# Weights of the first mixture rounded on GpSimd instead of ScalarE, with half of their low parts, a unit's third division, and later writes of constant rows

## The chip, the cores and the metric

The kernel runs on one core of one Trainium2 chip. The metric is the device time of one execution in microseconds. A core has five engines with queues of their own, each worked off in order: TensorE (PE in the rows; PEld is its weight load), VectorE (DVE), ScalarE (ACT), GpSimd (POOL) and SyncE (SP), which issues nearly all DMAs here.

## The reference

Attention with a causal mask and a bias from running sums, 4 batches of 8 heads, 576 tokens, head size 64; then two feed-forward layers ("mixtures") on 2304 tokens, 512 to 2048 to 512. Shortened:

```python
def _attn_ref(q, k, v, s) -> np.ndarray:
    B, H, S, D = q.shape
    scale = 1.0 / np.sqrt(D)
    scores = scale * np.matmul(q, k.transpose(0, 1, 3, 2))
    causal = np.triu(np.ones((S, S), dtype=bool), k=1)
    s_pos = np.maximum(s, 0.0)
    cum = np.cumsum(s_pos, axis=-1)
    bias = -(cum[:, :, :, None] - cum[:, :, None, :])
    scores = np.where(causal, -1000000000.0, scores + np.minimum(bias, 0.0))
    scores = scores - np.max(scores, axis=-1, keepdims=True)
    attn = np.exp(scores)
    attn = attn / (np.sum(attn, axis=-1, keepdims=True) + 1e-09)
    return np.matmul(attn, v).astype(np.float32)
...
    x = np.ascontiguousarray(attn_out.transpose(0, 2, 1, 3)).reshape(B * S, H * D)
    h = x @ w_in                                    # first mixture
    x = (h * (1.0 / (1.0 + np.exp(-1.702 * h)))) @ w_out
    h = x @ w_in2                                   # second mixture
    r = np.maximum(h, 0.0)
    return (s2 * (r * r) + b2) @ w_out2
```

The weights `w_in`, `w_out` and so on arrive as 8-byte numbers.

## The kernel before

**Products in parts.** Each fp32 operand of a product is split in a rounded part and a rest ("low part"), both in a type that the TensorE multiplies in one pass; a product is then three: low by rounded, rounded by low, rounded by rounded. The scores and values of the first eight heads alone are multiplied in plain fp32.

**Weights.** A weight tile is 128 x 512 numbers; there are 16 of `wi` (f = 0 to 15) and 16 of `wo` for each mixture. `fetch_w` brings one as 8-byte words (512 KB) on SyncE's queue; `join_w` makes one 4-byte number of the two words, with one instruction on ScalarE (L139) and two on VectorE (L140 with one input, L141 with two); `split_w` rounds it (L149) and takes the low part (L150). `load_w` is all three, for the first mixture. The first mixture's `wi` is loaded two tiles after each attention step while the first eight heads run; its `wo` through a pool of three places (tag "pair").

**Units.** A batch's rows are cut at 320: a unit is one batch's first 320 rows (units 0 to 3) or last 256 rows (4 to 7), with 8 heads. Unit 0's heads (n below H = 8) are done first, alone. Then `run` does the mixture of a unit while it mixes in, at fixed places of the TensorE's order, the attention of the next unit: for a head the score products of up to three chunks of rows (`qk`, L277), a step later the transposes of the probabilities (`transposes`, L315), a step later the product with the values (`pv`, L336 or L342).

**A head.** `qk` takes the maxima on VectorE (L283) from PSUM, the exponentials on ScalarE (L289), reciprocals of the sums on VectorE (L293, L294), and then divides the chunks `x`: all but the last on GpSimd, the last on ScalarE. From head 8 on, `prep` splits a head's queries and keys into `hi` and `lo` (L254 to L257: ScalarE, VectorE, and the keys' low part on GpSimd, L257), with one buffer for `lo`, and the values (L262 and L263). The rows beside queries and keys, four for each, carry the running sums and constants. The first head gets them straight from SBUF; the others from a DRAM tile `rows_d`, which `setup` writes: `minus` and `root` hold constants, `high` and `low` the parts of the running sums.

**The mixture of a unit.** `split_x` splits the four tiles of a unit's x (L390, L391). `h_item` sums a tile of h (L404), with three PSUM places, takes tanh (L425, ScalarE), multiplies (L426, VectorE), rounds `g` (L430, ScalarE) and takes its low part (L431, GpSimd). `th` has two places. `y_item` multiplies `wo` and `g` (L444) for f = 0 to 7 and, later, 8 to 15. For unit 0 three h tiles are begun before the last head's `pv`.

**What sets the order.** The TensorE's order is written out (`attention_items` and `run`), and SyncE's in `setup` and the first eight heads. All other queues are ordered by a scheduler when the kernel is built; each engine then keeps that order. SyncE's issues take turns on eight semaphores, so an issue also waits for the one eight before it.

Of the kernel before, what the change touches and what calls it, by code (L numbers as in the profile page):

```python
# [12 lines left out]
AF = mybir.ActivationFunctionType  # L13
ALU = mybir.AluOpType
# [24 lines left out]
def f32(ap):  # L39
    return ap.bitcast(F32)  # L40
# [27 lines left out]
def fused_kernel(ctx: ExitStack, tc: tile.TileContext, qkT, vP, s, w1i, w1o, w2i, w2o, s2, b2, out):  # L68
    nc = tc.nc
    B, H, _, _ = qkT.shape  # L70
# [10 lines left out]
    first, second = [(0, 64), (64, 192), (192, 320)], [(320, 448), (448, 576)]  # L81
# [18 lines left out]
    rows_d = dram.tile([2, BH, 4, S], F32, name="rows_d")  # L100
# [7 lines left out]
    def scaled(engine, out, in_, scale=1.0):  # L108

        if engine is nc.scalar:  # L110
            nc.scalar.activation(out, in_, AF.Copy, scale=scale)
        elif engine is nc.gpsimd:
            nc.gpsimd.tensor_scalar(out=out, in0=in_, scalar1=scale, scalar2=0.0, op0=ALU.mult, op1=ALU.add)  # L113
        else:
            nc.vector.tensor_scalar(out=out, in0=in_, scalar1=scale, scalar2=None, op0=ALU.mult)  # L115

    def fetch_w(stage, src, f):

        pool, stage_tag, bufs = stage
        if src.dtype == F32:  # L120
            single = pool.tile([P, 2 * CM], F32, tag=stage_tag, name="single", bufs=bufs)[:, :CM]
            nc.sync.dma_start(single, src[f])
            return single
        pair = pool.tile([P, 2 * CM], U32, tag=stage_tag, name="pair", bufs=bufs)
        nc.sync.dma_start(pair, src[f].bitcast(U32))
        return pair

    def join_w(came):

        if came.dtype == F32:  # L130
            return came
        else:

            lower, upper = came[:, 0 : 2 * CM : 2], came[:, 1 : 2 * CM : 2]
            nc.scalar.activation(f32(upper), f32(upper), AF.Prelu, scale=2.0**-112, alpha=2.0**32)  # L139
            nc.vector.tensor_scalar(out=lower, in0=lower, scalar1=2.0**-29, scalar2=7.49, op0=ALU.mult, op1=ALU.min)  # L140
            nc.vector.scalar_tensor_tensor(  # L141
                out=lower, in0=upper, scalar=3, in1=lower, op0=ALU.logical_shift_left, op1=ALU.bitwise_or
            )
            return f32(lower)

    def split_w(single, tag, f):

        w = wp.tile([P, 2, CM], F32R, tag=tag, name=f"{tag}{f}")
        nc.scalar.activation(w[:, 0, :], single, AF.Copy)  # L149
        nc.vector.tensor_tensor(w[:, 1, :], single, f32(w[:, 0, :]), ALU.subtract)  # L150
        return w

    def load_w(stage, src, tag, f):
        return split_w(join_w(fetch_w(stage, src, f)), tag, f)


    with ExitStack() as p1:
# [15 lines left out]
        def setup():  # L173
            cum = gp.tile([P, 2 * NMAX], F32, tag="g", name="cum")[:BH, :S]
            nc.sync.dma_start(cum, s)
            root = gp.tile([P, 2 * NMAX], F32, tag="g", name="root")[:BH, :S]
            nc.gpsimd.memset(root, ROOT)
            minus = gp.tile([P, 2 * NMAX], F32, tag="g", name="minus")[:BH, :S]
            nc.gpsimd.memset(minus, -ROOT)
            prep_to(0)  # L180
            u, t = units[0], heads[0]
            raw = t["parts"][0][0]
            nc.sync.dma_start(raw[D + 2 : R, t["kc"]], minus[:2, : u.i1])
            nc.sync.dma_start(raw[D : D + 2, t["qc"]], root[:2, u.i0 : u.i1])
            for k in range(2):
                nc.sync.dma_start(rows_d[0, :, 2 + k, :], minus)
                nc.sync.dma_start(rows_d[1, :, k, :], root)
            zero = gp.tile([P, 2 * NMAX], F32, tag="g", name="zero")[:BH, :S]
            nc.vector.memset(zero, 0.0)
            pos = gp.tile([P, 2 * NMAX], F32, tag="g", name="pos")[:BH, :S]  # L190
            nc.vector.tensor_scalar(out=pos, in0=cum, scalar1=0.0, scalar2=None, op0=ALU.max)
            nc.vector.tensor_tensor_scan(cum, pos, zero, 0.0, ALU.add, ALU.add)
            high = gp.tile([P, 2 * NMAX], F32R, tag="g", name="high")[:BH, :S]
            nc.vector.tensor_copy(high, cum)
            low = gp.tile([P, 2 * NMAX], F32R, tag="g", name="low")[:BH, :S]
            nc.vector.tensor_tensor(low, cum, f32(high), ALU.subtract)

            for queue, k, part in ((nc.sync, 0, high), (nc.scalar, 1, low)):
                queue.dma_start(raw[D + k : D + k + 1, t["kc"]], f32(part)[:1, : u.i1])
                queue.dma_start(raw[D + 2 + k : D + 3 + k, t["qc"]], f32(part)[:1, u.i0 : u.i1])  # L200
            for k, part in enumerate((high, low)):
                nc.sync.dma_start(rows_d[0, :, k, :], f32(part))
                nc.sync.dma_start(rows_d[1, :, 2 + k, :], f32(part))

        ap, limit = None, 0
        size = {}
# [12 lines left out]
        def tile(shape, name, dtype=F32):  # L219
            return ap.tile([P, *shape], dtype, tag=name, name=name, bufs=size["bufs"][name])  # L220
# [45 lines left out]
        def qk(n, c):  # L266
            u, t = units[n // H], heads[n]
            a0, a1 = u.chunks[c]
            w = a1 - a0
            x = t["x"][c] = tile([size["keys"]], "x")  # L270
            pieces = [(0, a1)] if a1 <= 512 else [(0, a1 // 2), (a1 // 2, a1)]
            least = LARGEST
            for j0, j1 in pieces:
                ps = psS.tile([P, 512], F32, tag="s", name="ps")
                q0, k0 = t["qc"].start - u.i0, t["kc"].start
                for i, (part, rows) in enumerate(t["parts"]):
                    nc.tensor.matmul(  # L277
                        ps[:w, : j1 - j0], part[:rows, q0 + a0 : q0 + a1], part[:rows, k0 + j0 : k0 + j1],
                        start=(i == 0), stop=(i == len(t["parts"]) - 1),
                    )  # L280
                m = sp.tile([P, 1], F32, tag="m", name="m")

                nc.vector.tensor_tensor_reduce(  # L283
                    out=x[:w, j0:j1], in0=ps[:w, : j1 - j0], in1=mask[:w, WIDE - a0 + j0 : WIDE - a0 + j1],
                    scale=-1.0 / ROOT, scalar=least, op0=ALU.add, op1=ALU.min, accum_out=m[:w],
                )
                least = m[:w]
            tot = tots[n % len(tots)]
            nc.scalar.activation(x[:w, :a1], x[:w, :a1], AF.Exp, bias=least, scale=-1.0, accum_out=tot[:w, c : c + 1])  # L289
            last = len(u.chunks) - 1  # L290
            if c < last:
                return
            nc.vector.tensor_scalar(out=tot[:, : c + 1], in0=tot[:, : c + 1], scalar1=1e-9, scalar2=None, op0=ALU.add)  # L293
            nc.vector.reciprocal(tot[:, : c + 1], tot[:, : c + 1])  # L294
            for k, (b0, b1) in enumerate(u.chunks):
                engine = nc.scalar if k == last else nc.gpsimd
                scaled(engine, t["x"][k][: b1 - b0, :b1], t["x"][k][: b1 - b0, :b1], tot[: b1 - b0, k : k + 1])

        def transposes(n, g):
# [71 lines left out]
        def prep_to(n):  # L371
            while n_prep[0] <= min(n, limit - 1):
                prep(n_prep[0])
                n_prep[0] += 1

        def attend(item):
            _, kind, n, k = item
            if kind == "qk":
                if k == 0:
                    prep_to(n + 1)  # L380
                qk(n, k)
            elif kind == "t":
                transposes(n, k)
            else:
                pv(n)
# [252 lines left out]
    def split_next():  # L638
        k = n_split[0]
        if k < len(joined) - 1 or k == len(order) - 1:  # L640
            _, tag, f = order[k]
            (wi2 if tag == "wi" else wo2)[f] = split_w(joined[k], tag, f)
            n_split[0] += 1
            fetch_to(k + 1 + FETCHED)
# [68 lines left out]
```

## Time and profile before

| | us |
|---|---|
| median of 3 runs | 1056.9 (1056.1 to 1056.94) |
| span of the profiled execution | 1052.8 |
| TensorE busy in the span | 1015.6 (96%) |
| VectorE, ScalarE, GpSimd busy | 650.6, 535.8, 347.7 |

The profiled execution's own time isn't listed apart from its span; the median lies 4.1 us above the span, for what comes ahead of the first instruction and behind the last. A row of the timeline gives start, length, engine, line, operation, names of output and inputs and, in brackets, how long the engine had been idle and what ended that. Rows of the same kind that follow each other are merged ("x2").

### The profile page before, as it was taken

To read this page: it belongs to the slowest core of one execution; us is meant where nothing else is said; L and a number is where in the kernel's file an instruction comes from. 1 tells how busy PE (TensorE), PEld (TensorE's weight loads), DVE (VectorE), ACT (ScalarE), POOL (GpSimd) and SP (SyncE) were. 2 spreads that over 40 slices of the span, in tenths; PEclk is the share of its full clock that TensorE was granted. 3 is DMA by queue.
4 is the path that set the end of the run, shared out by engine and by line. 5 is a ranking of instruction groups with operands and counts; after the bars stand their busy time and mean duration, and the time that the engine had idled before them with its cause. 6 is when DMAs were issued, how large, how long until landed. Compare 5 with 4: busy or idle time off the path is not lost.

```text
span 1052.8 us, 17330 instructions
## 1 busy us (share of the span) xinstructions
PE 1015.6 (96%) x6216; PEld 909.6 (86%) x6216; DVE 650.6 (62%) x1441; ACT 535.8 (51%) x1252; POOL 347.7 (33%) x382
## 2 busy tenths in 40 slices
PE   5989999999999999999999999999999999999998
PEld 3459989999989999999999999788888888888887
DVE  4689877567467788778877579866422332232343
ACT  4888856646536646656656557544422322222222
POOL 1126535435335436435445235112410301111011
PEclk9998999999999999999999999999999999999999
DMA  5665331221042232222222084531300100100010
GB/s 178 217 236 182 120 97 56 65 81 44 6 129 71 67 105 72 83 92 72 84 74 68 21 300 134 167 101 41 110 1 1 65 1 1 46 1 1 1 40 21
DMA packets 39181, 85.51 MB, mean 81 GB/s; under 512 B 5660, under 2 KB 16536, under 8 KB 39096
## 3 DMA queue, kind: packets, MB, share of 16 engines
q1 hardware_dynamic: 38888, 84.27, 25.1%
q8 instruction: 49, 0.80, 0.3%
q14 instruction: 36, 0.29, 0.1%
q10 hardware_dynamic: 208, 0.13, 0.0%
HBM read 70.29 MB, written 10.03 MB: 76 GB/s over the span
## 4 chain that ended last, share of the span: by engine, by line
PE 78%; DVE 11%; ACT 4%; DMA 3%; issue 2%; SPq 1%; DVEq 0%; ACTq 0%
PE py L604 19%; PE ph L554 18%; PE py L444 14%; PE ph L404 14%; PE ps L277 4%; PE pst L315 4%; PE po L342 3%; DVE hi L115 3%; DMA pair<-w1i 2%; DVE x L283 1%; PE py L580 1%; ACT x L289 1%; DVE pair L141 1%; DVE pair L140 1%; PE po L336 1%
## 5 line engine op out<-in xcount | busy, mean ns | idle before, releaser
L404 PE MATMUL ph<-xT,wi 128*128 128x320 f32 (+1 forms) x1536 | 246.1, 305 | 5.6 <-ACT xT L390 2.5
L404 PEld LDWEIGHTS ph<-xT,wi 128*128 128x128 f32 x1536 | 217.0, 193 | 7.1 <-ACT xT L390 3.0
L444 PE MATMUL py<-g,wo 128*128 128x320 f32 (+1 forms) x1344 | 215.2, 304 | 0.0
L604 PE MATMUL py<-wo,g 128*128 128x512 f32 x864 | 208.1, 390 | 2.4 <-POOL g L563 2.4
L554 PE MATMUL ph<-xT,wi 128*128 128x512 f32 (+1 forms) x960 | 208.4, 368 | 0.0
L554 PEld LDWEIGHTS ph<-xT,wi 128*128 128x128 f32 x960 | 169.0, 188 | 31.0
L604 PEld LDWEIGHTS py<-wo,g 128*128 128x128 f32 x864 | 161.1, 188 | 36.2 <-POOL g L563 3.3
L444 PEld LDWEIGHTS py<-g,wo 128*128 128x128 f32 x1344 | 188.0, 189 | 0.9 <-POOL g L431 0.2
L558 DVE TENSOR_TENSOR r<-r 128x512 f32<-128x512 f32 (+1 forms) x80 | 53.6, 670 | 189.1 <-ACT r L557 188.9
L431 POOL TENSOR_TENSOR g<-th,g 128x320 fp32r<-128x320 f32 (+1 forms) x128 | 116.3, 909 | 128.9 <-ACT g L430 114.2
L563 POOL TENSOR_TENSOR g<-r,g 128x512 fp32r<-128x512 f32 (+1 forms) x40 | 48.6, 1216 | 306.3 <-PE py L604 174.9
L289 ACT ACTIVATE x<-x,m 64x64 f32<-64x64 f32 (+2 forms) x160 | 89.5, 560 | 100.2 <-DVE m L283 98.8
L557 ACT ACTIVATE r<-ph 128x512 f32<-128x512 f32 (+1 forms) x80 | 44.4, 555 | 147.7 <-PE ph L554 146.1
L257 POOL TENSOR_TENSOR lo<-raw,hi 64x576 fp32r<-64x576 f32 (+1 forms) x56 | 68.1, 1217 | 123.0 <-issue 57.2
L283 DVE CUSTOM_DVE_ANT_0 x<-ps,mask 64x64 f32<-64x64 f32 (+2 forms) x160 | 68.1, 426 | 52.2 <-PE ps L277 50.4
L315 PE MATMUL pst<-ident,x 128*128 128x128 f32 (+2 forms) x480 | 85.8, 287 | 9.9 <-DVE ph L324 8.1
L562 ACT ACTIVATE g<-r 128x512 fp32r<-128x512 f32 (+1 forms) x80 | 47.1, 589 | 91.9 <-DVE r L559 91.8
L113 POOL TENSOR_SCALAR x<-x,tot 64x64 f32<-64x64 f32 (+1 forms) x96 | 49.3, 520 | 91.3 <-DVE tot L294 71.4
L321 ACT ACTIVATE ph<-pst 64x256 fp32r<-64x256 f32 (+2 forms) x144 | 67.0, 473 | 20.6 <-PE pst L315 19.2
L315 PEld LDWEIGHTS pst<-ident,x 128*128 128x128 f32 (+2 forms) x480 | 54.8, 136 | 24.7 <-DVE ph L324 13.0
L425 ACT ACTIVATE th<-ph 128x320 f32<-128x320 f32 (+1 forms) x128 | 51.7, 404 | 45.5 <-PE ph L404 42.7
L426 DVE SCALAR_TENSOR_TENSOR th<-th,ph 128x320 f32<-128x320 f32 (+1 forms) x128 | 57.5, 449 | 22.5 <-ACT th L425 21.5
(71 smaller groups left out, 1334.8 us busy)
## 6 DMA issues: line engine op xcount, KB each, us to landing
raw<-qkT SPq DMA_DIRECT2D x32, 416.0 KB
pair<-w1o SPq DMA_DIRECT2D x16, 512.0 KB
pair<-w1i SPq DMA_DIRECT2D x16, 512.0 KB
pair<-w2i SPq DMA_DIRECT2D x16, 512.0 KB
pair<-w2o SPq DMA_DIRECT2D x16, 512.0 KB
raw<-qkT SPq DMA_DIRECT2D x24, 320.0 KB
vraw<-vP SPq DMA_DIRECT2D x16, 320.0 KB
out<-y SPq DMA_DIRECT2D x17, 256.0 KB
```

Source lines behind the costliest of these rows:

```text
L257: nc.gpsimd.tensor_tensor(lo[:D, kc], raw[:D, kc], f32(hi[:D, kc]), ALU.subtract)
L283: nc.vector.tensor_tensor_reduce(out=x[:w, j0:j1], in0=ps[:w, : j1 - j0], in1=mask[:w, WIDE - a0 + j0 : WIDE - a0 + j1], scale=-1.0 / ROOT ...
L289: nc.scalar.activation(x[:w, :a1], x[:w, :a1], AF.Exp, bias=least, scale=-1.0, accum_out=tot[:w, c : c + 1])
L315: nc.tensor.transpose(ps[: j1 - j0, at : at + a1 - a0], t["x"][c][: a1 - a0, j0:j1], ident[: a1 - a0, : a1 - a0])
L321: nc.scalar.activation(t["ph"][:rows, base:end], ps[:rows, :m], AF.Copy)
L404: nc.tensor.matmul(ph[:, :n], wi[f][:, a, cc * P : (cc + 1) * P], x[cc][:, b, :n], start=(k == 0), stop=(k == 3 * NC - 1),)
L426: nc.vector.scalar_tensor_tensor(out=th[:, :n], in0=th[:, :n], scalar=1.0, in1=ph[:, :n], op0=ALU.add, op1=ALU.mult)
L431: nc.gpsimd.tensor_tensor(g[:, 1, :n], th[:, :n], f32(g[:, 0, :n]), ALU.subtract)
L444: nc.tensor.matmul(py[:, :n], wo[f][:, a, wc], g_t[ui, f][:, b, :n], start=(k == 0), stop=(k == 3 * G - 1))
L554: nc.tensor.matmul(ph[:, :n], wi2[f][:, a, wc], x[cc][:, b, :n], start=(k == 0), stop=(k == 3 * NC - 1))
L558: nc.vector.tensor_tensor(r, r, r, ALU.mult)
L604: nc.tensor.matmul(py[t], g2[k][a][:, t * P : (t + 1) * P], wo2[k][:, b, :], start=(k == 0 and i == 0), stop=(k == NF - 1 and i == 2),)
```

## The change

`split_w` takes a pair of engines. For the first mixture `load_w` hands it GpSimd for the rounding of every tile, and for the low part GpSimd where f is odd and VectorE where it is even. The second mixture's calls keep ScalarE and VectorE. For heads below 8 the third division of `qk` goes to GpSimd too. The four writes of constant rows to `rows_d` move behind those of `high` and `low`, two after each.

```diff
--- before.py
+++ after.py
@@ -143,15 +143,16 @@
             )
             return f32(lower)
 
-    def split_w(single, tag, f):
+    def split_w(single, tag, f, engines=(nc.scalar, nc.vector)):
 
         w = wp.tile([P, 2, CM], F32R, tag=tag, name=f"{tag}{f}")
-        nc.scalar.activation(w[:, 0, :], single, AF.Copy)
-        nc.vector.tensor_tensor(w[:, 1, :], single, f32(w[:, 0, :]), ALU.subtract)
+        first, rest = engines
+        scaled(first, w[:, 0, :], single)
+        rest.tensor_tensor(w[:, 1, :], single, f32(w[:, 0, :]), ALU.subtract)
         return w
 
     def load_w(stage, src, tag, f):
-        return split_w(join_w(fetch_w(stage, src, f)), tag, f)
+        return split_w(join_w(fetch_w(stage, src, f)), tag, f, (nc.gpsimd, nc.gpsimd if f % 2 else nc.vector))
 
 
     with ExitStack() as p1:
@@ -182,9 +183,6 @@
             raw = t["parts"][0][0]
             nc.sync.dma_start(raw[D + 2 : R, t["kc"]], minus[:2, : u.i1])
             nc.sync.dma_start(raw[D : D + 2, t["qc"]], root[:2, u.i0 : u.i1])
-            for k in range(2):
-                nc.sync.dma_start(rows_d[0, :, 2 + k, :], minus)
-                nc.sync.dma_start(rows_d[1, :, k, :], root)
             zero = gp.tile([P, 2 * NMAX], F32, tag="g", name="zero")[:BH, :S]
             nc.vector.memset(zero, 0.0)
             pos = gp.tile([P, 2 * NMAX], F32, tag="g", name="pos")[:BH, :S]
@@ -201,6 +199,8 @@
             for k, part in enumerate((high, low)):
                 nc.sync.dma_start(rows_d[0, :, k, :], f32(part))
                 nc.sync.dma_start(rows_d[1, :, 2 + k, :], f32(part))
+                nc.sync.dma_start(rows_d[0, :, 2 + k, :], minus)
+                nc.sync.dma_start(rows_d[1, :, k, :], root)
 
         ap, limit = None, 0
         size = {}
@@ -293,7 +293,7 @@
             nc.vector.tensor_scalar(out=tot[:, : c + 1], in0=tot[:, : c + 1], scalar1=1e-9, scalar2=None, op0=ALU.add)
             nc.vector.reciprocal(tot[:, : c + 1], tot[:, : c + 1])
             for k, (b0, b1) in enumerate(u.chunks):
-                engine = nc.scalar if k == last else nc.gpsimd
+                engine = nc.scalar if k == last and n >= H else nc.gpsimd
                 scaled(engine, t["x"][k][: b1 - b0, :b1], t["x"][k][: b1 - b0, :b1], tot[: b1 - b0, k : k + 1])
 
         def transposes(n, g):
```

In SyncE's row this is what stands between the constants of the first head and the last write to `rows_d`, before:

```order
L183 DMA raw_119<-minus_117 2x320
L184 DMA raw_119<-root_115 2x320
L186 DMA rows_d_81<-minus_117 32x576
L187 DMA rows_d_81<-root_115 32x576
L186 DMA rows_d_81<-minus_117 32x576
L187 DMA rows_d_81<-root_115 32x576
L199 DMA raw_119<-high_134 1x16x20
L200 DMA raw_119<-high_134 1x16x20
L202 DMA rows_d_81<-high_134 32x576
L203 DMA rows_d_81<-high_134 32x576
L202 DMA rows_d_81<-low_136 32x576
L203 DMA rows_d_81<-low_136 32x576
```

and now:

```order
L184 DMA raw_119<-minus_117 2x320
L185 DMA raw_119<-root_115 2x320
L197 DMA raw_119<-high_130 1x16x20
L198 DMA raw_119<-high_130 1x16x20
L200 DMA rows_d_81<-high_130 32x576
L201 DMA rows_d_81<-high_130 32x576
L202 DMA rows_d_81<-minus_117 32x576
L203 DMA rows_d_81<-root_115 32x576
L200 DMA rows_d_81<-low_132 32x576
L201 DMA rows_d_81<-low_132 32x576
L202 DMA rows_d_81<-minus_117 32x576
L203 DMA rows_d_81<-root_115 32x576
```

The sends of `high` to the first head have moved ahead of all writes to `rows_d`; two of the four constant writes are now the last.

VectorE, from the first of the last four `wi` tiles that come (wi12 to wi15, `pair_587`, `595`, `620`, `628`) to the last x tile of unit 0 (`xT_681`), before, the last 12 rows of 18:

```order
L140 TENSOR_SCALAR pair_620<-pair_620 128x512
L141 SCALAR_TENSOR_TENSOR pair_595<-pair_595 128x512
L140 TENSOR_SCALAR pair_628<-pair_628 128x512
L141 SCALAR_TENSOR_TENSOR pair_620<-pair_620 128x512
L150 TENSOR_TENSOR wi12_592<-pair_587,wi12_592 128x512
L141 SCALAR_TENSOR_TENSOR pair_628<-pair_628 128x512
L150 TENSOR_TENSOR wi13_600<-pair_595,wi13_600 128x512
L150 TENSOR_TENSOR wi14_625<-pair_620,wi14_625 128x512
L140 TENSOR_SCALAR pair_759<-pair_759 128x512
L150 TENSOR_TENSOR wi15_633<-pair_628,wi15_633 128x512
L141 SCALAR_TENSOR_TENSOR pair_759<-pair_759 128x512
L391 TENSOR_TENSOR xT_681<-xraw_607,xT_681 128x320
```

and now, all of it:

```order
L140 TENSOR_SCALAR pair_587<-pair_587 128x512
L151 TENSOR_TENSOR wo0_689<-pair_684,wo0_689 128x512
L141 SCALAR_TENSOR_TENSOR pair_587<-pair_587 128x512
L140 TENSOR_SCALAR pair_595<-pair_595 128x512
L151 TENSOR_TENSOR wo2_740<-pair_735,wo2_740 128x512
L141 SCALAR_TENSOR_TENSOR pair_595<-pair_595 128x512
L140 TENSOR_SCALAR pair_620<-pair_620 128x512
L151 TENSOR_TENSOR wi12_592<-pair_587,wi12_592 128x512
L141 SCALAR_TENSOR_TENSOR pair_620<-pair_620 128x512
L140 TENSOR_SCALAR pair_628<-pair_628 128x512
L141 SCALAR_TENSOR_TENSOR pair_628<-pair_628 128x512
L391 TENSOR_TENSOR xT_681<-xraw_607,xT_681 128x320
```

The low parts of wo1, wi13 and wi15 have gone to GpSimd, and wi14's and one join of `wo` stand behind the x tile.

GpSimd, from the keys' low part of the 13th head (`lo_1106`) to that of the 14th (`lo_1211`), in the stretch in which unit 0's y products run, before:

```order
L257 TENSOR_TENSOR lo_1106<-raw_1101,hi_1105 64x320
L113 TENSOR_SCALAR v_854<-vraw_844 128x3x2x64
L431 TENSOR_TENSOR g_1048<-th_1045,g_1048 128x320
L263 TENSOR_TENSOR v_854<-vraw_844,v_854 128x3x128
L113 TENSOR_SCALAR x_1116<-x_1116,tot3_74 64x64
L113 TENSOR_SCALAR x_1128<-x_1128,tot3_74 128x192
L257 TENSOR_TENSOR lo_1211<-raw_1208,hi_1210 64x320
```

and now:

```order
L257 TENSOR_TENSOR lo_1106<-raw_1101,hi_1105 64x320
L113 TENSOR_SCALAR wo11_1377<-pair_1372 128x512
L113 TENSOR_SCALAR v_854<-vraw_844 128x3x2x64
L151 TENSOR_TENSOR wo11_1377<-pair_1372,wo11_1377 128x512
L263 TENSOR_TENSOR v_854<-vraw_844,v_854 128x3x128
L113 TENSOR_SCALAR wo12_1420<-pair_1415 128x512
L113 TENSOR_SCALAR x_1116<-x_1116,tot3_74 64x64
L113 TENSOR_SCALAR x_1128<-x_1128,tot3_74 128x192
L113 TENSOR_SCALAR wo13_1453<-pair_1448 128x512
L151 TENSOR_TENSOR wo13_1453<-pair_1448,wo13_1453 128x512
L257 TENSOR_TENSOR lo_1211<-raw_1208,hi_1210 64x320
```

Three roundings and two low parts of weights have come between, and a `g` (`g_1048`) stands ahead of the piece now.

## Rows read from the trace of the kernel before

**Rows 1.** Windows, TensorE: stretch, length, busy (instructions), granted clock, DMA share, GB/s
```profile
65.00:94.00 29.00, 24.57 (x138) 0.88 0.70 249
120.00:640.00 520.00, 507.51 (x3848) 1.00 0.27 83
```

**Rows 2.** Timeline, TensorE: start us, us, engine, line, operation, [idle before <-releaser]
```profile
10.19 2.46 PE L277 MATMUL ps<-raw 68*64 68x64 f32 x6 [10.19 <-DMA raw<-high]
14.11 2.45 PE L277 MATMUL ps<-raw 68*64 68x64 f32 x6 [1.47 <-DVE tot L293]
...
63.76 1.67 PE L315 MATMUL pst<-ident,x 64*64 64x64 f32 x6 [1.00 <-POOL x L113]
...
73.97 0.41 PE L404 MATMUL ph<-xT,wi 128*128 128x320 f32 x1 [2.14 <-ACT xT L390]
74.79 1.70 PE L404 MATMUL ph<-xT,wi 128*128 128x320 f32 x5 [0.40 <-DVE xT L391]
...
93.89 0.85 PE L404 MATMUL ph<-xT,wi 128*128 128x320 f32 x4 [1.89 <-DVE th L426]
...
118.01 0.20 PE L277 MATMUL ps<-lo 68*64 68x64 f32 x1
```

**Rows 3.** Windows of 2 us, TensorE, columns as in rows 1
```profile
74.00:76.00 2.00, 1.60 (x5) 0.57 0.00 0
80.00:82.00 2.00, 2.00 (x12) 0.72 0.80 265
96.00:98.00 2.00, 2.00 (x10) 0.50 0.57 231
```

**Rows 4.** Timeline of SyncE's DMA issues
```profile
5.21 0.42 SPq L186 DMA_DIRECT2D rows_d<-minus  x1
7.28 0.30 SPq L187 DMA_DIRECT2D rows_d<-root  x1
7.70 0.60 SPq L199 DMA_DIRECT2D raw<-high  x1
...
12.29 0.24 SPq L234 DMA_DIRECT2D raw<-rows_d  x1
```

**Rows 5.** Groups up to 180 us: busy us, mean ns, then idle before
```profile
L150 DVE TENSOR_TENSOR wo<-pair,wo 128x512 fp32r<-128x512 f32 x16 | 11.8, 743 | 0.1
...
L149 ACT ACTIVATE wo<-pair 128x512 fp32r<-128x512 f32 x16 | 10.3, 660 | 0.6 <-DVE pair L141 0.6
```

**Rows 6.** Timeline, GpSimd
```profile
14.47 0.71 POOL L113 TENSOR_SCALAR x<-x,tot 64x64 f32<-64x64 f32 x2 [11.20 <-DVE tot L294]
...
60.95 0.51 POOL L113 TENSOR_SCALAR v<-vraw 128x384 fp32r<-128x384 f32 x1 [2.55 <-DMA vraw<-vP]
...
62.64 1.47 POOL L113 TENSOR_SCALAR x<-x,tot 64x64 f32<-64x64 f32 x2
...
83.79 1.32 POOL L431 TENSOR_TENSOR g<-th,g 128x320 fp32r<-128x320 f32 x1 [2.01 <-ACT g L430]
...
86.98 0.87 POOL L431 TENSOR_TENSOR g<-th,g 128x320 fp32r<-128x320 f32 x1
...
113.15 1.12 POOL L257 TENSOR_TENSOR lo<-raw,hi 64x320 fp32r<-64x320 f32 x1 [1.84 <-PE ps L277]
...
785.70 1.29 POOL L563 TENSOR_TENSOR g<-r,g 128x512 fp32r<-128x512 f32 x1 [9.59 <-PE py L604]
```

**Rows 7.** Timeline, VectorE
```profile
28.98 0.43 DVE L140 TENSOR_SCALAR pair<-pair 128x512 uint32<-128x512 uint32 x1 [0.29 <-DMA pair<-w1o]
29.32 0.69 DVE L150 TENSOR_TENSOR wi<-pair,wi 128x512 fp32r<-128x512 f32 x1
...
64.28 0.43 DVE L140 TENSOR_SCALAR pair<-pair 128x512 uint32<-128x512 uint32 x1 [0.67 <-DMA pair<-w1i]
...
74.25 0.48 DVE L391 TENSOR_TENSOR xT<-xraw,xT 128x320 fp32r<-128x320 f32 x1
...
88.33 1.10 DVE L140 TENSOR_SCALAR pair<-pair 128x512 uint32<-128x512 uint32 x1
```

## The prediction

> **What bounds the kernel now.** I read the busy time of the TensorE by stretch first. From 120 us on it is nearly full, 507.5 of 520 us up to 640 [rows 1], and the order of every engine there is the same after the change, so only what shifts the start of that stretch can count: the first 120 us. Up to 65 us the TensorE does the attention of the first unit; from 65 to 94 it is busy 24.6 of 29 us at a mean clock of 0.88 [rows 1]. Next I read its own timeline for what ended each wait [rows 2]: 10.19 us for the rows of the first head, 1.47 for the second head, 1.00 at 63.76 for GpSimd's divisions, 2.14 and 0.40 at 74 for the two parts of the last x tile, 1.89 at 93.89 for a `th`. Last I read the granted clock: it is 0.57 in 74 to 76, 0.72 in 80 to 82 and 0.50 in 96 to 98 [rows 3], that is at 1.2 GHz for a time after the two longest waits, at full speed after those of 1.00 and 1.47 us. From 74.6 to 81.1 this costs some 3 us, from 94.5 to 98 some 1.7 us (half of each).
>
> The waits at 74 and 94 stand in the stretch in which VectorE and ScalarE work off the weights, two instructions of 512 columns on each of the two engines for joining and splitting every tile. So there is some 2.5 + 3 + 1.9 + 1.7 = 9 us to win, if nothing takes these engines' place.
>
> **The constant rows.** In the queue of SyncE the third write of constant rows is out at 5.63 (5.21 + 0.42), the fourth starts only at 7.28 (it waits for the first w1o tile to land), and `high` of the first head follows at 7.70 [rows 4]. Afterwards `high` is sent before them, at 5.6 or sooner, so the first matmul could start some 2.1 us sooner. But the second head waits for rows from DRAM, and these wait for all eight writes, the constant ones now among the last. I count the issues: eight writes of 0.4 us each from 7.28 (the second of them, one of `high`, now waits for that tile) less the one already out: 7.28 + 7 x 0.42 = 10.2, and the read that now comes at 12.29 stood behind six issues and one landing after 7.28, two of the issues longer ones of 0.6 [rows 4]; without these two it comes at some 11.7. **Gain 0.6 us** (bounds 0 and 2.1); a wait for the second head stays.
>
> **The first unit's third division** goes from ScalarE to GpSimd, behind the other two. GpSimd's pair takes 0.71 us alone [rows 6], the third some 0.5 more (320 columns, against 0.51 us for 384 at 60.95 [rows 6]). A head's transposes stand a step behind its scores in the TensorE's order, and the only wait for a division in the whole list is the last head's [rows 2], so the other heads pay nothing, except that the sixth head's reciprocal now stands behind the seventh's last maximum on VectorE: up to 0.5 us of wait. The last head's pair stood behind the value tile and ran at 62.64, 1.47 us long [rows 6]; it is now in front of it. That removes the 1.00 us at 63.76. Together **a gain of 0.5 us** (bounds -0.5 and 1.0).
>
> **The weights.** 32 roundings leave ScalarE, 0.66 us each, and 16 low parts leave VectorE, 0.74 us each with what they waited [rows 5]. GpSimd gets both. A rounding of 128x512 on GpSimd is not in the trace; the nearest row is the value tile's, 0.51 us for 384 columns [rows 6], so 0.61 by columns beyond a small fixed part (bounds 0.51 and 0.68, in proportion). A low part of 512 columns is the row at 785.70, 1.29 us [rows 6]. So GpSimd gets 32 x 0.61 + 16 x 1.29 = 40 us, 25 us of it (20 tiles) between 60 and 120.
>
> What could hide this is GpSimd's idle time; what spoils it is VectorE. An instruction of VectorE with SBUF inputs and one of GpSimd lengthen each other: the L140 at 88.33 takes 1.10 us against 0.43 at 28.98 [rows 7], the `g` at 83.79 takes 1.32 against 0.87 at 86.98 [rows 6]. The second pair gives the price: 0.45 us of delay per low part of 0.60 us that falls on it (0.69 less the overlap of 0.09, as L140's 0.43 against 0.34 from start to start [rows 7]), so three quarters of VectorE's time is added to GpSimd's when both are backed up.
>
> *At 74 us.* From the landing of wi12 at 64.28 [rows 7], which comes about 0.6 us sooner, VectorE has before the x tile: four joins (0.34 + 0.60) and three low parts, 5.6 us, where it had five joins and seven low parts, 8.9. Alone it would be done by 69.3, and the x tile would wait for the TensorE's own last product, which ends at 73.97 - 2.14 = 71.8 [rows 2], less the 1.1 us gained so far, and for ScalarE's copy and rounding of it. But GpSimd has wo1's low part, three or four roundings and wi13's low part at the same time, 1.29 x 2 + 0.61 x 3 = 4.4 us, and they alternate: 63.7 + 5.6 + 4.4 = 73.7, and 0.48 for the x tile: 74.2. The TensorE goes on at 74.2 instead of 74.79, **0.6 us sooner**; the two gains above end in this wait, and the clock falls again. Bounds: 71.7 (GpSimd never in the way: 3 us sooner, and 3 more if the clock then holds), 75.5 (all four last roundings and low parts ahead too).
>
> *At 92 to 118 us.* GpSimd's row now decides when the next heads' low parts (`lo`, L257) are there. From wi15's rounding to `lo` of the 14th head it has 10 `g` and 5 `lo` at 0.85, 12 roundings at 0.61, 7 low parts at 1.29, 4 pairs of divisions at 0.71, and a value tile with its low part at 0.51 + 1.04: 12.8 + 7.3 + 9.0 + 2.8 + 1.6 = 33.5 us, where it was 17.2. VectorE has 12 joins, 6 low parts and 4 x 0.43 for L256 beside it, 11.3 + 3.6 + 1.7 = 16.6, of which three quarters, 12.5 us, come on top. Starting at 73.2 (between 70.5 and 74) this ends at 73.2 + 46 = 119.2. Before, that `lo` ran at 113.15 for 1.12 us [rows 6] and the TensorE took it at 118.01 [rows 2]: 3.7 us of slack, used up. The TensorE gets there 0.6 us sooner, at 117.4, so it waits 1.8 us, in some smaller waits (the third division, a value tile's low part) rather than one. Net: 119.2 - 118.0 = **1.2 us later than before**. Bounds: 0.6 sooner (no wait), and 5.2 later (all of VectorE's 16.6 added, from 73.2). After that two roundings and one low part are left, the load falls to what it was, and the TensorE is full again. The w1o tiles 8 to 15 are used only in the second half of the unit's y products, and don't bind.
>
> The Trainium skill, "SBUF — State Buffer", section "Who interferes with whom", says that VectorE, with two SBUF inputs or in a 2-port mode, and GpSimd exclude each other for the whole instruction. Nothing above uses it; the rows at 83.79 and 88.33 agree in kind, with three quarters instead of all.
>
> **The sum**, on the profiled execution: 1052.8 us of span, 4.1 us short of the median of 1056.9, which lie around the span and which I leave as they are. Span 1052.8 + 1.2 = 1054.0, time 1058.1.
>
> **The rivals.**
> 1. *GpSimd is no bottleneck; the relief of ScalarE and VectorE shows.* For it: 8.9 us of VectorE's row before the x tile become 5.6, and 0.66 us of ScalarE ahead of the same tile are gone. Then the TensorE goes on at 72 to 73 without the clock falling: 2.3 + 3.1 = 5.4 us less, some of it given back at 92 to 118. 1053.0 (1051.5 to 1054.8). Against: the sum of 46 us, which such an early start does not change.
> 2. *Only the early gains stay.* The queue at 92 to 118 just fits: 0.6 us less, 1056.3, together with the forecast the middle of the range.
> 3. *GpSimd becomes the bound outright.* If the two engines exclude each other fully, and the row starts at 74, `lo` is there at 74 + 33.5 + 16.6 = 124.1, 6 us late: 1063. It ends on the slow side from the point where the sum passes 118 + 2.1, that is where GpSimd's row takes over 47 us from 73.2. By the page named above it is this case.
> 4. *It costs the clock.* The waits at GpSimd come as one of 2 us or more, as the two that were followed by 1.2 GHz [rows 2, 3]: 1.7 us to the forecast, 1059.8.
>
> **How the numbers follow.** Forecast 0.36 (its own range 1056.5 to 1060), rival 1 0.26, rival 2 0.16, rival 3 0.10, rival 4 0.12. A measurement of this kernel can tell about 0.2% from no change, 2.1 us: faster is under 1054.8, slower over 1059.0. Faster: rival 1, 0.26. Slower: rivals 3 and 4, 0.22, and a quarter of the forecast, 0.09. Within: the rest, 0.43. The range leaves out half of rival 1 and some of rival 3: 1053.0 to 1062.0.
>
> **What would show it.** Right: the first matmul before 9 us and the second head near 13.5; no wait for a division at 63; the TensorE going on at 74 with the clock at 1.2 GHz for some us; GpSimd full from 62 to 120, with `lo` of the 14th head ending near 119; waits of the TensorE for GpSimd or `lo` between 100 and 120. Wrong: the TensorE going on at 72 at full clock, GpSimd idle in 75 to 115, or its roundings taking far from 0.61 us.

## The result and the profile after

The changed kernel takes 1069.0 us (1068.8 to 1069.4), the kernel before, run beside it, 1056.5 (1054.3 to 1056.9): a ratio of 1.0133, interval 1.0111 to 1.0154. It is slower by 12.5 us; the prediction said 1058.1 with an upper end of 1062.0. The span of its profiled execution is 1067.3 us, 14.5 more. In every run of this case that lists both, the time is 1.7 to 2.3 us longer than the span; so the 4.1 us between median and span before are mostly not time around the span: that profile is of an execution of some 1054.6 us (an estimate, the span and 1.8), under the median, and 14.5 us is the difference of two single executions.

The same windows of the TensorE as in [rows 1], with 94 to 120 us added (stretch, length, busy, granted clock, DMA share, GB/s):

```profile
65.00:94.00 29.00, 20.49 (x104) 0.82 0.47 164
94.00:120.00 26.00, 18.91 (x118) 0.93 0.48 150
120.00:640.00 520.00, 507.50 (x3832) 1.00 0.27 85
```

From 120 us on nothing changed (507.50 us busy, 507.51 before). Between 65 and 94 us 4.1 us of busy time are gone, and between 94 and 120, where the TensorE was busy without a break before (26.00), 7.1. What ended its waits there (columns as in [rows 2]):

```profile
8.45 1.38 PE L277 MATMUL ps<-raw 68*64 68x64 f32 x4 [8.45 <-DMA raw<-low]
...
13.67 2.45 PE L277 MATMUL ps<-raw 68*64 68x64 f32 x6 [2.18 <-DMA raw<-rows_d]
...
64.48 0.42 PE L315 MATMUL pst<-ident,x 128*64 128x128 f32 x1 [0.43 <-POOL x L113]
65.26 1.06 PE L315 MATMUL pst<-ident,x 128*64 128x128 f32 x4 [0.35 <-POOL x L113]
...
74.11 0.42 PE L404 MATMUL ph<-xT,wi 128*128 128x320 f32 x1 [1.57 <-ACT xT L390]
77.71 1.70 PE L404 MATMUL ph<-xT,wi 128*128 128x320 f32 x5 [3.18 <-DVE xT L391]
...
88.61 2.50 PE L404 MATMUL ph<-xT,wi 128*128 128x320 f32 x8 [3.50 <-DVE th L426]
...
99.91 2.02 PE L404 MATMUL ph<-xT,wi 128*128 128x320 f32 x12 [2.10 <-DVE th L426]
...
115.67 0.63 PE L277 MATMUL ps<-lo 68*128 68x320 f32 x1 [4.13 <-DVE m L283]
```

From 77 us on the large waits (3.18, 3.50, 2.10, 4.13) are all for VectorE, the engine that was relieved; none is for GpSimd or `lo`, as the prediction had it. VectorE's groups between 60 and 120 us (busy us, mean ns, idle before), first of the kernel before, then after:

```profile
L140 DVE TENSOR_SCALAR pair<-pair 128x512 uint32<-128x512 uint32 x17 | 9.2, 545 | 1.1 <-DMA pair<-w1i 0.9
L426 DVE SCALAR_TENSOR_TENSOR th<-th,ph 128x320 f32<-128x320 f32 x10 | 4.7, 474 | 0.0
L293 DVE TENSOR_SCALAR tot<-tot 128x3 f32<-128x3 f32 x5 | 1.6, 325 | 0.0
```

```profile
L140 DVE TENSOR_SCALAR pair<-pair 128x512 uint32<-128x512 uint32 x14 | 14.4, 1031 | 0.7 <-DMA pair<-w1o 0.6
L151 DVE TENSOR_TENSOR wo<-pair,wo 128x512 fp32r<-128x512 f32 x6 | 6.3, 1054 | 2.6 <-POOL wo L113 2.6
L426 DVE SCALAR_TENSOR_TENSOR th<-th,ph 128x320 f32<-128x320 f32 x10 | 4.8, 479 | 0.1
L293 DVE TENSOR_SCALAR tot<-tot 128x3 f32<-128x3 f32 x5 | 4.5, 901 | 0.0
```

The same instruction L140 takes 1031 ns on average instead of 545, and 14 of them are done instead of 17. The addition to 3 columns (L293) nearly triples. L426, one of whose inputs is in PSUM, keeps its time. L151 (L150 before) also waited 2.6 us for one rounding. Single rows show what lengthens them, here VectorE and then GpSimd:

```profile
60.81 1.97 DVE L293 TENSOR_SCALAR tot<-tot 128x3 f32<-128x3 f32 x1
...
67.45 1.15 DVE L151 TENSOR_TENSOR wo<-pair,wo 128x512 fp32r<-128x512 f32 x1 [2.63 <-POOL wo L113]
...
77.17 0.48 DVE L391 TENSOR_TENSOR xT<-xraw,xT 128x320 fp32r<-128x320 f32 x1
...
84.79 2.73 DVE L140 TENSOR_SCALAR pair<-pair 128x512 uint32<-128x512 uint32 x1
87.55 0.49 DVE L256 TENSOR_TENSOR hi<-raw,hi 64x320 fp32r<-64x320 f32 x1
88.06 0.49 DVE L426 SCALAR_TENSOR_TENSOR th<-th,ph 128x320 f32<-128x320 f32 x1
```

```profile
60.41 1.09 POOL L257 TENSOR_TENSOR lo<-raw,hi 64x320 fp32r<-64x320 f32 x1
61.47 1.28 POOL L151 TENSOR_TENSOR wi<-pair,wi 128x512 fp32r<-128x512 f32 x1
63.17 2.04 POOL L113 TENSOR_SCALAR x<-x,tot 64x64 f32<-64x64 f32 x3 [0.42 <-DVE tot L294]
65.18 0.50 POOL L113 TENSOR_SCALAR v<-vraw 128x384 fp32r<-128x384 f32 x1
65.77 1.00 POOL L263 TENSOR_TENSOR v<-vraw,v 128x384 fp32r<-128x384 f32 x1
66.74 2.36 POOL L113 TENSOR_SCALAR wo<-pair 128x512 fp32r<-128x512 f32 x3
...
84.28 1.69 POOL L113 TENSOR_SCALAR wo<-pair 128x512 fp32r<-128x512 f32 x2
85.94 1.29 POOL L151 TENSOR_TENSOR wo<-pair,wo 128x512 fp32r<-128x512 f32 x1
...
126.93 1.32 POOL L257 TENSOR_TENSOR lo<-raw,hi 64x320 fp32r<-64x320 f32 x1
```

The L140 of 84.79 ends at 87.52, 0.3 us after the end of GpSimd's row (85.94 + 1.29 = 87.23); the `th` behind it in VectorE's order comes at 88.06, and the TensorE, which waits for it, goes on at 88.61 after 3.50 us. The L293 of 60.81 ends at 62.78, just as the low part of 61.47 does (62.75), and with it the last head's divisions move to 63.17.

To compare the runs I use one place that all kernels pass: the first maximum of a head (L283, 64x64), which stands in VectorE's order behind the same product of the TensorE. The TensorE's order is the same in all of them. Between the 2nd and the 14th head's I add up three things of VectorE: its **own work** (each instruction at the 20% quantile of its form, that is operation and shapes, over the ten executions), its **stretch** (what the instructions took beyond that) and its **idle** time (gaps over 0.15 us); beside it GpSimd's busy time. The rows of one engine overlap slightly, so the three add up to 10 to 13 us more than the interval. The last column is how late the 22nd head is against the kernel before; from the 15th head on this hardly changes. Each row is one execution, and one can lie some 3 us off its kernel's median: e6's took 1069.1 us (median 1066.2), e9's 1051.9 (1054.6).

| kernel | 2nd to 14th head, us | own | stretch | idle | GpSimd | 22nd head |
|---|---|---|---|---|---|---|
| before | 104.8 | 90.1 | 10.0 | 16.5 | 34.9 | 0 |
| after | 118.0 | 79.2 | 32.5 | 17.0 | 81.2 | +12.6 |
| e11, weights alone | 116.2 | 79.2 | 31.1 | 16.2 | 78.5 | +12.3 |
| e1, roundings on ScalarE | 113.4 | 79.2 | 23.5 | 21.5 | 58.8 | +9.2 |
| e2, low parts on VectorE | 116.8 | 90.1 | 21.0 | 18.2 | 63.3 | +12.3 |
| e5, only `wi` on GpSimd | 109.4 | 84.7 | 24.8 | 11.7 | 61.3 | +3.6 |
| e6, only `wo` on GpSimd | 116.2 | 84.7 | 23.4 | 19.1 | 57.9 | +11.7 |
| e7, idle work, 160 columns | 119.2 | 90.1 | 23.9 | 17.1 | 97.5 | +15.1 |
| e8, idle work, 4 columns | 110.3 | 90.1 | 10.0 | 21.5 | 79.9 | +5.2 |
| e9, rows and divisions | 102.7 | 90.1 | 11.7 | 13.8 | 39.7 | -3.2 |

The change took 10.9 us of own work off VectorE and put 22.5 us of stretch on it: a net 11.6 of the 13.2 us by which the interval grew.

### The profile page after: what moved, and what is told of

It reads as the page before. It is cut to its first block, busy times and chain, and to the rows that moved or that the text cites. A ratio compares the mean times of both kernels' runs of the same rounds, so it can differ in the third digit from the quotient of the medians.

```text
span 1067.3 us, 17371 instructions
## 1 busy us (share of the span) xinstructions
PE 1018.3 (95%) x6216; PEld 910.4 (85%) x6216; DVE 662.9 (62%) x1425; ACT 515.4 (48%) x1212; POOL 395.0 (37%) x438
## 4 chain that ended last, share of the span: by engine, by line
PE 78%; DVE 13%; ACT 4%; DMA 3%; issue 2%; SPq 1%; POOL 0%; DVEq 0%; ACTq 0%; POOLq 0%
PE py L604 19%; PE ph L554 18%; PE ph L404 14%; PE py L444 14%; PE ps L277 4%; PE pst L315 4%; PE po L342 3%; DVE hi L115 3%; DVE pair L140 2%; DVE x L283 1%; DVE pair L141 1%; PE py L580 1%; ACT x L289 1%; DMA pair<-w1i 1%; DMA pair<-w1o 1%
## 5 line engine op out<-in xcount | busy, mean ns | idle before, releaser
L257 POOL TENSOR_TENSOR lo<-raw,hi 64x576 fp32r<-64x576 f32 (+1 forms) x56 | 68.5, 1224 | 116.2 <-PE ps L277 52.4
L283 DVE CUSTOM_DVE_ANT_0 x<-ps,mask 64x64 f32<-64x64 f32 (+2 forms) x160 | 67.8, 426 | 53.6 <-PE ps L277 51.7
L113 POOL TENSOR_SCALAR x<-x,tot 64x64 f32<-64x64 f32 (+3 forms) x104 | 52.1, 509 | 62.1 <-DVE tot L294 46.3
L430 ACT ACTIVATE g<-th 128x320 fp32r<-128x320 f32 (+1 forms) x128 | 56.4, 440 | 33.3 <-DVE th L426 32.7
```

Of the source, the lines that this page charges most:

```text
L257: nc.gpsimd.tensor_tensor(lo[:D, kc], raw[:D, kc], f32(hi[:D, kc]), ALU.subtract)
L283: nc.vector.tensor_tensor_reduce(out=x[:w, j0:j1], in0=ps[:w, : j1 - j0], in1=mask[:w, WIDE - a0 + j0 : WIDE - a0 + j1], scale=-1.0 / ROOT ...
L430: nc.scalar.activation(g[:, 0, :n], th[:, :n], AF.Copy)
```

## The experiments

My theory (A) after the result: VectorE's instructions stand still while GpSimd's run, and VectorE's row, not GpSimd's, becomes late. The rivals: (B) VectorE waits, in its order, for roundings that are queued on GpSimd; (C) the constant rows or the divisions cost it; (D) the scheduler's other order on VectorE costs it.

**One part back or one part alone (e1 to e4).** In `load_w`, against the changed kernel:

```
-        return split_w(..., (nc.gpsimd, nc.gpsimd if f % 2 else nc.vector))
+        return split_w(..., (nc.scalar, nc.gpsimd if f % 2 else nc.vector))   # e1
+        return split_w(..., (nc.gpsimd, nc.vector))                           # e2
```

e3 is the kernel before with the constant rows' writes moved alone, e4 the kernel before with `if k == last and n >= H` alone.

e1, expected: 

> The changed kernel with the 32 roundings of the first mixture's weights back on ScalarE; the 16 odd low parts, the third divisions and the constant rows stay as changed. GpSimd loses 32 x 0.64 = 20 us of the 41 us that the change gave it. Theory A (VectorE's instructions stand still while GpSimd's run, so the loss goes with GpSimd's busy time before 120 us): about half of the 12.5 us of loss is left, 1060 to 1065 us, and VectorE's one-input instructions in 60 to 120 us still take well over their 545 ns of before. Theory B (VectorE waits in its own order for roundings that are queued behind other work on GpSimd): the roundings are gone from that queue, so all of the loss goes, 1055 to 1057 us. Theory C (divisions or constant rows): nothing changes, 1068 to 1070 us.

e2, expected: 

> The changed kernel with all 32 low parts back on VectorE; the roundings stay on GpSimd. GpSimd loses 16 x 1.29 = 21 us, VectorE gets 16 x 0.66 = 11 us back. Theory A (standing still beside GpSimd): GpSimd's busy time before 120 us is about that of the run with the roundings on ScalarE, so the time is near it, 1060 to 1066 us. Theory B (VectorE waits in order for roundings): the roundings stand before every low part, all of them on VectorE now, so the loss stays, 1067 to 1072 us. Theory C (divisions or constant rows): 1068 to 1070 us.

e3, expected: 

> The kernel before with the constant rows written later and nothing else. My step on it: the second head starts 0.4 us sooner (13.67 us in the changed kernel, 14.11 before), 1056.0 us, within 0.5 us of before. Theory C1 (the later rows cost the time): 1066 to 1069 us.

e4, expected: 

> The kernel before with the third division of the first eight heads on GpSimd and nothing else. My step on it: a wait of 1.00 us at 63.76 us goes, up to 0.5 us comes, 1056.0 us, within 1 us of before. Theory C2 (the divisions cost the time): eight instructions of 1.2 us where three quarters of that stands in the path, 1060 us or more.

Measured against before: e1 1064.8 us, ratio 1.0101 (1.0086 to 1.0116); e2 1068.3, 1.0132 (1.0117 to 1.0147); e3 1057.9, 1.0036 (1.0016 to 1.0055); e4 1055.6, 1.0005 (0.9989 to 1.0021). C falls: neither small part costs more than 0.4% (where e3's 0.36% comes from the traces don't show; its 22nd head is 0.5 us early, and e9 below, which holds the same part, is not slower). B falls as the whole cause: with no rounding on GpSimd e1 still loses 10 us. The traces show how small its share is: between the 2nd and the 14th head VectorE waits 2.6 us for a rounding in the changed kernel, 0.9 in e2 and none in e11 (below), which is as late. But e2 came where B had put it, and above A's 1060 to 1066: A's halves don't add, each half alone costs nearly all. The table says why. In e2 VectorE is given no relief (own work 90.1), so less stretch (21.0) does the same harm; e1 has the relief, but a stretch of 23.5. One of its rows, VectorE and then GpSimd:

```profile
91.92 3.06 DVE L141 SCALAR_TENSOR_TENSOR pair<-pair 128x512 uint32<-128x512 uint32 x1
```

```profile
91.27 1.06 POOL L257 TENSOR_TENSOR lo<-raw,hi 64x320 fp32r<-64x320 f32 x1
92.29 1.31 POOL L151 TENSOR_TENSOR wo<-pair,wo 128x512 fp32r<-128x512 f32 x1
93.56 0.87 POOL L431 TENSOR_TENSOR g<-th,g 128x320 fp32r<-128x320 f32 x1
```

An instruction of 0.68 us takes 3.06: it stands still for three instructions of GpSimd in a row, until 94.43, and ends 0.55 us later.

**Idle work on GpSimd (e7, e8).** The kernel before, with work on GpSimd that nobody reads:

```
         w = split_w(join_w(fetch_w(stage, src, f)), tag, f)
+        for c in (0, 160, 320): scaled(nc.gpsimd, idle[:, :160], f32(w[:, 0, c : c + 160]))
+        for c in (0, 160, 320) if f % 2 else (): nc.gpsimd.tensor_tensor(idle[:, :160], ..., ALU.subtract)
         return w                          # e8: 4 columns for 160
```

e7, expected: 

> The kernel before, nothing of it moved or removed; behind each of the first mixture's weight tiles GpSimd also scales three pieces of 128x160 of the rounded tile into a scratch tile (for odd f it also subtracts the low part, three pieces), and nobody reads the scratch. GpSimd gets about as much as in the changed kernel, 32 x 0.65 + 16 x 1.3 = 42 us, but no instruction of another engine waits for it. Theory A (VectorE's instructions stand still beside GpSimd's): in the four runs so far VectorE's instructions grew by 0.3 to 0.5 us for each us added on GpSimd, so 13 to 21 us here, of which nothing is taken off VectorE again: 1066 to 1076 us. Theory B (the loss is the waiting for roundings): none here, 1055 to 1058 us. Theory D (the scheduler's other order on VectorE costs it): the order is nearly that of before, 1055 to 1058 us.

e8, expected: 

> As the run with idle work on GpSimd, with the same instructions in number and place, but each on 4 columns instead of 160. All theories but one: 1055 to 1058 us. If instructions on GpSimd cost VectorE by their number and not by their time, it is as slow as its long sister.

Measured: e7 1070.4 us, 1.0129 (1.0106 to 1.0152); e8 1061.6, 1.0050 (1.0036 to 1.0064). e7 loses as much as the change, though no engine reads any of the added work, and VectorE keeps its order but for 36 of 1441 instructions (e4, where 147 stand elsewhere, loses nothing): D falls, and the loss needs no waiting for roundings. The stretch rises from 10.0 to 23.9. e8 came 3.6 us above its expectation and turned out the better control for it: its short instructions keep GpSimd busy, 79.9 us against 81.2 after the change, but VectorE's stretch stays at 10.0. So between these runs the stretch goes with how long GpSimd's instructions run, not with their number or its busy time. What e8 loses is another thing, GpSimd's own queue; its GpSimd, ScalarE and VectorE rows:

```profile
81.83 0.74 POOL L113 TENSOR_SCALAR idle<-wo 128x4 fp32r<-128x4 f32 x3
82.53 0.87 POOL L431 TENSOR_TENSOR g<-th,g 128x320 fp32r<-128x320 f32 x1
```

```profile
83.44 0.44 ACT L425 ACTIVATE th<-ph 128x320 f32<-128x320 f32 x1 [2.67 <-POOL g L431]
```

```profile
83.90 0.49 DVE L426 SCALAR_TENSOR_TENSOR th<-th,ph 128x320 f32<-128x320 f32 x1 [2.77 <-ACT th L425]
```

A `g` stands behind idle work, frees its place of `th` late, and ScalarE and VectorE wait. e7 has some of this too (ScalarE waits 1.9 us there for `g`, 5.3 in e8, between 60 and 130 us), so not all that it loses is stretch. In the changed kernel this chain does not show: there GpSimd itself waits for ScalarE's `g`.

**Where it hurts (e5, e6).** Against the changed kernel, GpSimd's part for one of the two kinds of tile only:

```
+        ... if tag == "wi" else (nc.scalar, nc.vector))   # e5; e6: "wo"
```

e5, expected: 

> The changed kernel with the wo tiles treated as before (rounded on ScalarE, low parts on VectorE); only the wi tiles, which are loaded beside the first eight heads, go to GpSimd. Theory A: VectorE has some 16 us of idle time between 10 and 60 us, so standing still there costs little, 1055 to 1060 us. Theory B: it waits for the wi roundings there too, but not in 65 to 120 us, 1057 to 1061 us.

e6, expected: 

> The mirror of the last run: the wi tiles as before, only the wo tiles go to GpSimd. Theory A: the loss arises where VectorE has no idle time, between 65 and 120 us, so most of the 12.5 us is here, 1064 to 1069 us. If the wi tiles carry the loss (they run late and push the rest), 1056 to 1060 us.

Measured: e5 1060.1 us, 1.0037 (1.0025 to 1.0050); e6 1066.2, 1.0097 (1.0072 to 1.0122); in the medians the two add up to the change (both keep the rows and divisions, which e9 below shows to cost nothing). The stretch is about the same (24.8 and 23.4), but e5 has 17.8 of it before the 9th head, where VectorE had idle time to lose (16.5 to 11.7 us), and e6 has 16.1 of it between the 9th and the 14th, where VectorE was idle for 0.5 us in 41.8 before. That `wo` costs more than `wi` is as A expected, and e6 is in its range; e5 lies 0.1 us above A's range and inside B's, but its VectorE waits for no rounding.

**The rest of the split (e9, e11).** e9 is the changed kernel with `load_w` as before; e11 is the kernel before with the weights' part alone.

e9, expected: 

> The changed kernel without its weights part: constant rows later and third divisions on GpSimd, weights as before. If the two small parts add (each moved the heads by 0.5 to 0.9 us and neither moved the median by more than 0.4%), 1055 to 1057 us; the lead at the ninth head may reach 4 us and is given back by 120 us, as in the runs with one part each. If they hurt each other, or carry the loss only together, over 1060 us. If the lead is kept to the end, 1052 us, and the version would beat both kernels.

e11, expected: 

> The kernel before with the weights part of the change alone (32 roundings and 16 odd low parts on GpSimd). Theory A: this is the loss, all of it: 1066 to 1071 us. If the loss needs the third divisions or the later rows beside it, under 1064 us.

Measured: e9 1054.6 us, 0.9996 (0.9983 to 1.0009); e11 1068.1, 1.0117 (1.0100 to 1.0134). The weights are the loss, whole, as far as the intervals tell. The granted clock between the 2nd and the 14th head was 0.78 in e11 and e2 and 0.94 in the changed kernel, and all three end 12.3 to 12.6 us late, so the clock there is not what costs the time. e9's 9th head is 5.5 us early and its 14th 2.8; VectorE was idle for only 0.8 us between them, which is the likely reason for losing half of the lead. What is left of it its median doesn't show beyond doubt, so it doesn't beat the kernel before.

**The price by itself (e10, e12).** Probes with nothing of the reference's work in them.

e10, expected: 

> Nothing of the reference's work is done (the output is filled with zeros); the time says nothing, the rows do. Six kinds of VectorE instruction, with the shapes of this kernel, run first by themselves, then beside a row of four low parts on GpSimd (128x512, 1.29 us each alone), then beside a row of six roundings (0.64 us each alone). Each stage starts with one instruction from PSUM so that GpSimd is under way. If GpSimd holds the way until its row has a gap (the 2.7 to 3.1 us rows of the changed kernel and of the run with ScalarE's roundings), the first SBUF-only instruction of a stage takes several us, up to the whole row of some 5 or 4 us, and the rest of them their normal time. If the two engines take turns, each of four takes its own time plus about one GpSimd instruction, 1.7 to 2.0 us beside low parts. Instructions that read PSUM, and the reciprocal of 3 columns, keep their time (474 to 484 and 174 ns in both kernels) in either case; the 3-column addition does not (1.97 us at 60.81 us of the changed kernel).

VectorE's rows of e10, several like ones drawn together (x4, x8); up to 22 us alone, then beside four low parts on GpSimd, from 59 us beside six roundings:

```profile
6.76 1.81 DVE L87 TENSOR_SCALAR pair<-pair 128x512 uint32<-128x512 uint32 x4
...
8.95 2.87 DVE L90 SCALAR_TENSOR_TENSOR pair<-pair 128x512 uint32<-128x512 uint32 x4
...
15.45 1.59 DVE L98 TENSOR_SCALAR tot<-tot 128x3 f32<-128x3 f32 x8
...
23.07 5.48 DVE L87 TENSOR_SCALAR pair<-pair 128x512 uint32<-128x512 uint32 x4
...
28.94 6.58 DVE L90 SCALAR_TENSOR_TENSOR pair<-pair 128x512 uint32<-128x512 uint32 x4
...
42.88 5.29 DVE L98 TENSOR_SCALAR tot<-tot 128x3 f32<-128x3 f32 x8
...
48.55 1.65 DVE L101 RECIPROCAL tot<-tot 128x3 f32<-128x3 f32 x8
...
53.71 3.62 DVE L104 SCALAR_TENSOR_TENSOR vd<-va,acc 128x320 f32<-128x320 f32 x7
...
59.67 2.92 DVE L87 TENSOR_SCALAR pair<-pair 128x512 uint32<-128x512 uint32 x4
```

GpSimd beside L87 of 23.07, L90 of 28.94 and the reciprocals (L101):

```profile
22.79 5.47 POOL L107 TENSOR_TENSOR gc<-ga,gb 128x512 f32<-128x512 f32 x4 [22.35 <-DVE gb L113]
28.70 6.28 POOL L107 TENSOR_TENSOR gc<-ga,gb 128x512 f32<-128x512 f32 x4 [0.44 <-DVE gb L113]
...
48.31 5.28 POOL L107 TENSOR_TENSOR gc<-ga,gb 128x512 f32<-128x512 f32 x4 [0.37 <-DVE gb L113]
```

A one-input instruction (L87) costs 1.37 us beside low parts instead of 0.45, and GpSimd's row grows from 5.28 to 5.47; a two-input one (L90) costs 1.64 instead of 0.72, and GpSimd's row becomes 6.28. They take turns, one instruction each, at less than the 1.7 to 2.0 us expected. The delay falls on VectorE first: some 0.9 us for every instruction that meets a low part, whatever its own length (of the eight additions to 3 columns, L98, four do), and GpSimd pays 0.05 us for a one-input and 0.25 for a two-input one. Beside roundings, which are half as long, VectorE's delay is smaller: 0.28 us for each L87 (2.92 for 1.81). The reciprocals (1.64 alone) and instructions from PSUM (L104, 3.61 alone) keep their time.

e12, expected: 

> Again nothing of the reference's work is done (zeros are written). In the first probe a GpSimd row whose instructions all write one tile left 0.08 us between them (22.79 + 1.27, next at 24.14), and every SBUF-only VectorE instruction got its turn after one of them, 1.27 to 1.64 us each; in the whole kernels the rows of GpSimd that held a VectorE instruction for 2.7 to 3.1 us followed each other with an overlap of 0.04 us. Here the rows (4 low parts, then 8 roundings) run first with one output tile and then with four in turn. If the gap lets VectorE in: as before with one tile; with four tiles the first VectorE instruction takes up to the whole row, 5 us, and the rest their own time. If GpSimd always gives way after one instruction: the same figures both times, and the long holds of the whole kernels have another cause, which stays open.

With four output tiles GpSimd's instructions followed each other without a gap, and yet VectorE got its turn after each. VectorE's two-input row of e12 and the last three of the four low parts beside it:

```profile
65.15 6.59 DVE L90 SCALAR_TENSOR_TENSOR pair<-pair 128x512 uint32<-128x512 uint32 x4
```

```profile
66.14 5.05 POOL L107 TENSOR_TENSOR g<-ga,gb 128x512 f32<-128x512 f32 x3
```

All four took between 1.58 and 1.64 us. So the gap is not what decides. Why single instructions of the whole kernels stand still for two or three of GpSimd's stays open; in the changed kernel there are four with over 1.3 us of stretch before 130 us, 7.6 us in all, so most of its stretch lies in shorter delays. In e6 there are six, 12.5 us in all, more than half of its stretch: the probes' price doesn't cover those.

## Why the prediction was wrong

**Step by step.** *The constant rows*: right. The first matmul starts at 8.45 (10.19 in [rows 2]) and the second head at 13.67 instead of 14.11, still behind the rows from DRAM: 0.44 us where 0.6 was forecast. *The third division*: the wait of 1.00 us before 63.76 [rows 2] did not go; there are two of 0.43 and 0.35, later (and one of 0.41 at 52.08, inside the 0.5 allowed for), because the divisions' reciprocal stood behind the L293 that GpSimd held for 1.97 us. Without the weights' part (e9) the lead is kept up to the 9th head. *GpSimd's prices*: right, 0.64 us for a rounding (85.34 to 85.98 in the trace; 0.61 forecast), 1.29 for a low part.

*At 74 us* the forecast was 74.2, and the TensorE went on at 77.71, 2.9 us later than before; the other 9.7 of the 12.6 us came behind it. VectorE did what the step counted, four joins and three low parts; they took from 64.24 to 77.17, 12.9 us for 5.6 of own work, and the step allowed 4.4 on top. Of the 3 us missing, most is an order that the step left out: GpSimd was not free at 63.7, it had the divisions and the value tile in front of the roundings until 66.7, and the first low part on VectorE waited 2.63 us for its rounding. Here rival theory B has its one place.

*At 92 to 118 us* lies the step that failed: "three quarters of VectorE's time is added to GpSimd's when both are backed up", and with it "GpSimd's row now decides". The price was taken from GpSimd's side of the pair (the `g` of 83.79 in [rows 6]) and added to GpSimd's row alone; the other side, the L140 of 88.33 that took 1.10 instead of 0.43 [rows 7], was quoted beside it and never charged to VectorE. It is the larger one: beside low parts 0.9 us an instruction on VectorE, 0.05 to 0.25 on GpSimd (e10). So VectorE's row, nearly without idle time there before, became the late one: the change relieved it of 10.9 us and stretched it by 22.5. GpSimd was not full as forecast (46.1 us busy of 60 to 120), and its `lo` of the 14th head ended at 128.25, not 119.2, because its one buffer came free only with the TensorE's late products of the head before, not the other way about.

**The rivals.** Rival 3 (full exclusion) named the right mechanism with the right sign, and its time, 1063, was short for the same reason: it too added everything to GpSimd's row. The rule it rested on, from the Trainium skill, "SBUF — State Buffer", section "Who interferes with whom", lets whichever instruction comes first have the shared ports for its whole length. e10 agrees in kind, for two-input instructions, for one-input ones such as L87 and for additions to 3 columns. In size it agrees on VectorE's side alone, whose instruction ended only after the GpSimd instruction that it met; GpSimd lost 0.05 to 0.25 us to VectorE instructions of 0.45 and 0.72, so the two rows took less than the sum that full exclusion would give (5.48 us, where 1.81 and 5.28 add up to 7.09). Rival 4 (the clock) is a small part: after the waits at 77, 88 and 115 the clock falls to 1.2 GHz for a few us as in [rows 3], 0.82 on average between 65 and 94 us against 0.88, and 0.93 in both kernels between 94 and 120. Rivals 1 and 2 fell with the x tile at 77.

## What to carry to other kernels

Where VectorE has two inputs in SBUF, or does a one-input addition or scaling from SBUF to SBUF, work moved to GpSimd is not simply moved off VectorE: each of its instructions that met a 128x512 low part lost 0.9 us here, more than the 0.7 us of a low part that it was spared; one that met a rounding lost 0.28 in the probe. Charge the contention to both rows and ask which of them has idle time: the same stretch cost 4 us where VectorE idled and 10 us where it didn't. Instructions that read one operand from PSUM kept their time, so work that must go to GpSimd may do less harm beside those; no run here tried that in a whole kernel.

## What I had not expected of the hardware

- An addition to 128x3 on VectorE loses as much beside GpSimd as an instruction of 512 columns: 0.9 us beside a low part in e10; in the changed kernel one took 1.97 us, 0.17 alone. The reciprocal of the same 3 columns next to it keeps its 0.17.
- Single VectorE instructions stood still for two or three GpSimd instructions in a row (1.97 us for two, 2.73 and 3.06 for three); in the probes turns were strict. The reason for the difference stays open.
- A GpSimd instruction of 4 columns (0.19 us alone, at 83.37 us of e8) took 0.35 to 0.39 us on average beside VectorE's work, so the waiting goes both ways.
